# Other places in the order of work for three token pieces and one early load, in a bucket-attention and rational feed-forward kernel

## The chip, the core and the metric

The kernel runs on one core of a Trainium2 chip. The metric is device microseconds for one execution, lower being better. The five engines of the core each work through their own instructions in order: PE (TensorE, the matrix multiplications), DVE (VectorE), ACT (ScalarE), POOL (GpSimd) and SP (SyncE), which here does nothing but issue DMAs. They meet only through semaphores, so an instruction that waits holds up everything behind it on its engine.

## The reference: what is computed

Attention among tokens that fall into the same hash bucket, then a feed-forward layer with a rational function in its middle. Everything is float32.

```python
# q, k, v: 4 batches x 8 heads x 768 tokens x 64;  proj: 64 x 6
q_bits = (q @ proj > 0); k_bits = (k @ proj > 0)
q_bucket = sum(q_bits * 2**arange(6)); k_bucket = sum(k_bits * 2**arange(6))
scores = q @ k.T / sqrt(64)
scores = where(q_bucket[:, None] == k_bucket[None, :], scores, -1e9)
attn = exp(scores - max(scores)); attn = attn / (sum(attn) + 1e-9)
x = (attn @ v)                       # heads side by side: 3072 tokens x 512
# feed-forward, w_in: 512 x 2048, w_out: 2048 x 512
h = x @ w_in
P = a[0] + a[1]*h + a[2]*h**2 + a[3]*h**3
Q = 1 + abs(b[0])*abs(h) + abs(b[1])*h**2
out = (P / (Q + 1e-6)) @ w_out       # 3072 x 512
```

## The kernel before, in words

**Precision.** A float32 operand of a matmul is split into a high part (a rounded copy, made by ACT) and a low part (the operand less its high part, made by DVE or POOL), and the products of high with high, high with low and low with high are added up. Names ending in `1`, `_hi`, `h` are high parts, those ending in `2`, `lo`, `_lo`, `l` low ones.

**Attention.** The 32 heads are handled as 16 pairs (0 to 15), two heads on the 128 partitions. For a pair, `load` brings q and k (`qkf<-qT`, `qkf<-kT`, 384 KB each) into a tile that two pairs share in turn; `high` and `low` split them; `second_low` and `second_high` copy the halves to where the second of the two score matmuls reads them, eight DMAs of 192 KB within the chip; `bits` multiplies q and k by the projection for two pairs at once (`psb`, for pairs 2 and 3 in one go), and `penalties` and `maskrows` turn the bits into extra rows of q and k, so that the mask is part of the score product. `maxstep` (`psm` on PE, `m` on DVE) finds each query's largest score, `shift_turn` and `shift_rows` make it one more row. Then come twelve steps, `scores` (`pss` on PE, the exponential `E` on ACT, and running sums `acc` on POOL, for the last pair half of them on DVE) and, for six steps together, `values` (`psv`, 24 matmuls, which read all six exponentials). The results go to `x_d` in memory, the reciprocal sums to `r_d`.

**Weights.** Beside all this, `weights(0)` to `weights(31)` bring in w_in (even numbers) and w_out (odd ones) in blocks of 512 KB (`wr<-w_in`, `wr<-w_out`; 64-bit values, which ACT and DVE turn into float32) and split them; w_out's go back to memory as `wo_d`. The blocks 28 to 31 fall into the last two pairs.

**Feed-forward.** Tokens are taken in 6 blocks of 512. Each block's 512 features for 512 tokens are loaded in three pieces by `Tokens.load(t, c)`: pieces 0 and 1 are 768 wide, piece 2 is 512 wide. A piece takes four steps: DMAs for x and its reciprocal sums r (six for pieces 0 and 1, three for piece 2; all on SP); the multiplication `x<-x,r` on DVE; the high part `xh` on ACT; the low part `xl` on DVE. x and r lie in one buffer each (tags `lo0` and `lo1`, which `low` also uses during attention), so a piece's DMAs wait until the piece before has been read for the last time. `psh` and `pso` are the two products. The first block's pieces are made during the pairs 14 and 15; this change-over, from about 360 to 420 us, is called the seam here.

**Order.** Every engine keeps the program order. That order is written out in a table: each piece of work is entered under a number (12 times the pair plus a step with decimals), and the program is put out in rising numbers. The dictionaries `MID`, `FIRST` and `LAST` hold these numbers. `LAST["tokens"]` holds four numbers for each of the three pieces, counted from pair 15, `FIRST["load3"]` the one for the load of pair 3, counted from pair 0. No cost model or due time is at work when the program is built; moving a number moves the work past its neighbours on each engine that it uses.

```python
for g in sorted(plan):
    for f, args in plan[g]:
        f(*args)
```

Of the kernel before, what the change touches and what calls it, by code (L numbers as in the profile page):

```python
# [50 lines left out]
    maxima1=4.62, rate1=0.45, maxima2=9.5, rate2=0.82, high=[3.25, 3.53], low=[6.0, 7.3], bits=7.15, penalties=7.25,  # L51
    high_move=4.53, maskrows=8.2, second_low=4.25, second_high=4.35, load_v=4.78, group=2,
    values=[2.35, 2.65, 2.32, 2.35, 0.35, 0.61], values_out=3.02, high1=[-0.27, -5.58], low1=[11.24, 4.95],
    high_move1=20.05, load2=21.89, load3=4.5, penalties1=-6.57, maskrows1=3.69,
    weights=[[-5.7, 6.64, 6.7, 11.42, 12.19, 18.75, 21.75, 38.77, 44.13], [8.03, 9.04, 9.24, 11.12, 14.81, 15.27, 15.99, 17.91, 46.81]],
    warm=6, warms=[3, 3, 3, 1, 1, 1], maxima00=[-4.26, -2.29, -4.17, 1.67, -1.15, 2.77], shift00=[2.15, 4.99],
    shift0=[3.67, 3.44], ahead=3, scores=[[3.68, 3.82, 7.26], [6.03, 8.25, 12.4]], pen01=[4.77, 14.55], comp01=3.35,
# [3 lines left out]

LAST = dict(
    group=6, values=[0.28, 0.44], values_out=1.39, vout14=3.03,
    tokens=[[-11.0, -7.43, -6.5, -5.11], [-3.0, 0.9, 2.1, 3.83], [4.9, 8.5, 9.38, 9.53]], terms=7.05, ffn=[13.61, 16.09, 16.14],
    sums=16.96, wide=8, share=11, third=0, sums14=14.69, sumst14=22.46,
)
TINY = 2.0 ** -80
# [764 lines left out]
```

## Time and profile before

| | us |
|---|---|
| median of 3 runs | 942.82 (941.68 to 946.25) |
| the profiled execution itself | 940.38 |
| its span in the profile | 938.6 |
| PE busy | 924.1 (98%) |
| DVE busy | 840.5 (90%) |
| ACT busy | 647.0 (69%) |
| POOL busy | 436.0 (46%) |

The profile comes from one execution, and its times count from the start of the span. In the rows below, `out<-in` gives the tiles by the program's names, `xN` says how many instructions a row stands for, and a bracket at the end gives how long the engine sat idle before the row and what ended that. All instructions have one line number (93), as a helper records them; the tiles tell them apart. `SPq` rows are the issues of DMAs on SP's queue, not the transfers. A row with several instructions is a merged one: its start is that of the first, and its length runs to the modelled end of the last.

### The profile page before, as it was taken

What the parts mean: (1) busy time and instruction counts of PE and PEld (TensorE: products, weight loads), DVE (VectorE), ACT (ScalarE), POOL (GpSimd) and SP (SyncE); (2) the same over time, 40 slices, a digit from 0 to 9 for tenths busy, and PEclk for the clock granted to TensorE, in tenths of its full rate; (3) what the DMA queues carried; (4) which work ended last, traced back from release to release, by engine and by line L of the source; (5) the groups of instructions that cost most, each with busy time, mean ns of one, the idle gap of its engine ahead of it and who ended that gap; (6) DMA issues with size and microseconds to landing.
All of it is one profiled execution on the core that took longest, in us unless ns stands there. A gap on an engine that the chain in (4) does not pass through costs nothing.

```text
span 938.6 us, 13660 instructions
## 1 busy us (share of the span) xinstructions
PE 924.1 (98%) x4678; PEld 700.4 (75%) x4678; DVE 840.5 (90%) x1029; ACT 647.0 (69%) x1229; POOL 436.0 (46%) x362
## 2 busy tenths in 40 slices
PE   8899999999999999999999999999999999999997
PEld 4466766676766766568888888888888888888886
DVE  6699889888988897789998999899999999998996
ACT  6466767676776766777777676777687677667664
POOL 5467888888778776622222222222322322222222
PEclk9999999999999999999999999999999999999999
DMA  6667878777878776536401100210021002001001
GB/s 195 175 181 229 226 218 228 215 223 225 229 223 227 227 193 197 170 119 246 142 29 62 51 23 1 79 35 23 1 79 38 20 34 79 23 1 45 0 1 45
DMA packets 51242, 111.57 MB, mean 119 GB/s; under 512 B 9346, under 2 KB 20214, under 8 KB 51172
## 3 DMA queue, kind: packets, MB, share of 16 engines
q1 hardware_dynamic: 50740, 110.47, 39.6%
q8 instruction: 37, 0.61, 0.3%
q14 instruction: 33, 0.27, 0.1%
q10 hardware_dynamic: 432, 0.23, 0.1%
HBM read 56.82 MB, written 21.17 MB: 83 GB/s over the span
## 4 chain that ended last, share of the span: by engine, by line
PE 89%; DVE 5%; DMA 2%; ACT 1%; issue 1%; SPq 1%; ACTq 0%; DVEq 0%
PE psh L93 28%; PE pso L93 28%; PE pss L93 12%; PE psv L93 11%; PE psm L93 6%; DVE m L93 3%; PE psu L93 2%; PE psb L93 1%; DVE ws L93 1%; ACT E L93 1%; SPq L93 1%; DMA qkf<-kT 1%; DVE wr L93 1%; DVE lo L93 1%; DMA q<-q 1%
## 5 line engine op out<-in xcount | busy, mean ns | idle before, releaser
L93 POOL TENSOR_TENSOR gl<-c,gh 128x512 fp32r<-128x512 f32 x96 | 136.4, 1421 | 385.8 <-ACT gh L93 376.5
L93 ACT ACTIVATE E<-pss 128x384 f32<-128x384 f32 x384 | 167.4, 492 | 107.2 <-PE pss L93 91.0
L93 PE MATMUL pso<-wo,gh 128*128 128x512 f32 x768 | 235.6, 389 | 0.0
L93 DVE TENSOR_REDUCE m<-psm 128x1 f32<-128x768 f32 x192 | 179.3, 948 | 34.0 <-PE psm L93 31.0
L93 POOL TENSOR_TENSOR acc<-E,E 128x384 f32<-128x384 f32 x124 | 152.9, 1252 | 91.8 <-ACT E L93 91.6
L93 PE MATMUL pss<-q,k 128*128 128x384 f32 (+2 forms) x768 | 171.1, 347 | 0.3 <-ACT E L93 0.3
L93 PEld LDWEIGHTS pso<-wo,gh 128*128 128x128 f32 x768 | 144.2, 188 | 29.9
L93 PEld LDWEIGHTS pss<-q,k 128*128 128x128 f32 (+2 forms) x768 | 134.7, 190 | 28.9 <-issue 17.0
L93 ACT ACTIVATE h<-psh 128x512 f32<-128x512 f32 x96 | 57.4, 598 | 135.0 <-PE psh L93 134.8
L93 PE MATMUL psh<-xh,wi_hi 128*128 128x512 f32 x384 | 149.8, 390 | 0.0
L93 PE MATMUL psh<-xl,wi_hi 128*128 128x512 f32 x384 | 149.6, 390 | 0.0
L93 PE MATMUL psh<-xh,wi_lo 128*128 128x512 f32 x384 | 149.6, 390 | 0.0
L93 PE MATMUL pso<-wo,gl 128*128 128x512 f32 x384 | 148.6, 389 | 0.0
L93 POOL TENSOR_TENSOR acc<-acc,E 128x384 f32<-128x384 f32 x123 | 136.5, 1128 | 13.5 <-ACT E L93 13.4
L93 DVE SCALAR_TENSOR_TENSOR c<-c,ab,r 128x512 f32<-128x512 f32 x96 | 139.7, 1456 | 0.0
L93 PE MATMUL psv<-E,v 128*64 128x385 f32 x768 | 133.7, 492 | 1.6 <-ACT E L93 1.6
L93 PE MATMUL psm<-k,q 76*128 76x384 f32 (+1 forms) x384 | 102.5, 349 | 2.2 <-DVE m L93 1.0
L93 PEld LDWEIGHTS psv<-E,v 128*64 128x64 f32 x768 | 52.7, 137 | 68.3 <-issue 61.5
L93 DVE SCALAR_TENSOR_TENSOR w<-h,absb,w 128x512 f32<-128x512 f32 x96 | 72.8, 759 | 15.7 <-ACT w L93 15.4
L93 PEld LDWEIGHTS psh<-xh,wi_hi 128*128 128x128 f32 x384 | 72.1, 188 | 16.1 <-issue 1.2
L93 PEld LDWEIGHTS psh<-xh,wi_lo 128*128 128x128 f32 x384 | 72.1, 188 | 14.9
L93 PEld LDWEIGHTS pso<-wo,gl 128*128 128x128 f32 x384 | 72.1, 188 | 14.9
(78 smaller groups left out, 1217.7 us busy)
## 6 DMA issues: line engine op xcount, KB each, us to landing
q<-q SPq DMA_DIRECT2D x45, 192.0 KB
k<-k SPq DMA_DIRECT2D x45, 192.0 KB
wr<-w_in SPq DMA_DIRECT2D x16, 512.0 KB
wr<-w_out SPq DMA_DIRECT2D x16, 512.0 KB
wo_d<-wr SPq DMA_DIRECT2D x16, 512.0 KB
wo<-wo_d SPq DMA_DIRECT2D x16, 512.0 KB
qkf<-qT SPq DMA_DIRECT2D x16, 384.0 KB
qkf<-kT SPq DMA_DIRECT2D x16, 384.0 KB
```

What stands on the lines that cost most here:

```text
L93: return self.tc.keep_in_program_order(issue(*args, **kwargs))
```

## The change

Two sets of numbers in the table of the order.

The load of pair 3 moves from 4.5 to 3.8. On SP's queue its two DMAs stood behind pair 1's `second_low` and `second_high`; now they stand in front of these, directly behind the four DMAs of pair 1's mask rows.

The three token pieces of the first feed-forward block get new numbers for their steps (only the last step of piece 2 keeps its own). In the order of the program:

- piece 0: its DMAs, which stood before weight block 28, pair 15's `second_high` and pair 13's second store, now stand behind these and before pair 13's sums. Its multiplication moves on DVE behind two maximum steps and two steps of block 28; its `xh` on ACT behind the exponentials of pair 14's steps 6 to 9, block 28's high part and pair 14's first output; its `xl` on DVE behind `shift_turn` of pair 15, the low part of block 28 and a step of block 29.
- piece 1: its DMAs move behind pair 15's load of v, before block 30. Its multiplication moves from step 0 of pair 15 to step 3; its `xh` from before the high part of block 29 to behind block 30's two conversions, just before the exponential of pair 15's step 5; its `xl` behind that step's add and a step of block 30.
- piece 2: its DMAs, its multiplication, its `xh` and its `xl` keep their neighbours on each engine (the numbers differ, but no other work of the same engine lies between), except that its DMAs can start only once piece 1's `xl` has been done.

No instruction is added or taken away.

```diff
 FIRST = dict(
...
-    high_move1=20.05, load2=21.89, load3=4.5, penalties1=-6.57, maskrows1=3.69,
+    high_move1=20.05, load2=21.89, load3=3.8, penalties1=-6.57, maskrows1=3.69,
...
 LAST = dict(
     group=6, values=[0.28, 0.44], values_out=1.39, vout14=3.03,
-    tokens=[[-11.0, -7.43, -6.5, -5.11], [-3.0, 0.9, 2.1, 3.83], [4.9, 8.5, 9.38, 9.53]], terms=7.05, ffn=[13.61, 16.09, 16.14],
+    tokens=[[-7.43, -5.11, -2.83, -1.09], [-0.04, 3.83, 4.5, 5.2], [6.0, 9.38, 9.45, 9.53]], terms=7.05, ffn=[13.61, 16.09, 16.14],
```

## The prediction

> **What bounds the kernel now.** I read the page first, then busy time by stretch, then the engines' timelines at the two places the change touches.
>
> ```profile
> span 938.6 us, 13660 instructions
> PE 924.1 (98%) x4678; PEld 700.4 (75%) x4678; DVE 840.5 (90%) x1029; ACT 647.0 (69%) x1229; POOL 436.0 (46%) x362
> ```
>
> PE is busy for 98% of the span, so only its 14.5 us of gaps can be won, and what every gap drags behind it. The busy time by stretch says where they lie:
>
> ```profile
> 0.00:50.00 50.00, 43.97 (x222) 24.38 (x222) 30.06 (x46) 27.03 (x46) 24.12 (x31) 1.00 0.66 191
> ...
> 200.00:250.00 50.00, 50.00 (x313) 34.20 (x313) 45.69 (x55) 36.01 (x82) 40.17 (x35) 1.00 0.80 233
> ...
> 380.00:400.00 20.00, 18.86 (x112) 11.62 (x111) 13.61 (x18) 14.39 (x34) 12.14 (x11) 1.00 0.57 184
> ```
>
> Columns: stretch, length, then busy us (count) of PE, PE's weight loads, DVE, ACT, POOL, then granted clock, DMA share, GB/s. The gaps are in the first 50 us and at the seam around 380 to 400, where attention passes into the feed-forward part; each of the two edits lies in one of them. In between PE is full, so what it gains early should arrive at the end undiminished.
>
> **Part 1, the load of pair 3 (load3, 4.5 to 3.8).** PE's timeline in pair 0:
>
> ```profile
> 33.92 0.84 PE L93 MATMUL psb<-qkf,prj 128*32 128x384 f32 x4
> ...
> 38.58 1.48 PE L93 MATMUL psb<-qkf,prj 128*32 128x384 f32 x10 [1.61 <-DMA qkf<-kT]
> 39.99 1.51 PE L93 MATMUL psv<-E,v 128*64 128x385 f32 x8
> ```
>
> These 16 matmuls make the bucket bits of pairs 2 and 3 together, and wait twice for pair 3's q and k. Here they hold PE from 33.92 to 39.99, 6.07 us; undisturbed, in the chain of waits, they take 1.29:
>
> ```profile
> 82.89 1.29 PE psb L93 x16
> ```
>
> So 6.07 - 1.29 = 4.78 us is the most this part can give. SP's queue, in its order of issue:
>
> ```profile
> 26.23 1.17 SPq L93 DMA_DIRECT2D q<-lo  x2
> ...
> 30.01 1.43 SPq L93 DMA_DIRECT2D k<-k  x2
> 31.54 0.94 SPq L93 DMA_DIRECT2D qkf<-qT  x1
> 32.53 0.81 SPq L93 DMA_DIRECT2D qkf<-kT  x1
> ```
>
> The two loads move ahead of eight copies within the chip (pair 1's low and high halves, two to a row from 26.23 to 31.44), from 31.54 to 26.23, 5.31 us sooner. Their tile is free by then: its last reader is POOL's subtraction of pair 1.
>
> ```profile
> 20.98 1.84 POOL L93 TENSOR_TENSOR lo<-qkf,q 128x768 fp32r<-128x768 f32 x1
> ```
>
> When do they land? Before, k was issued at 32.53 and released PE at 38.58, 6.05 us later, with eight copies in front. Issued at 27.22 (26.23 plus the 0.99 between the two), even that long a time gives 33.27, before PE asks at 33.92; a shorter one changes nothing. Both waits go. The eight copies start 1.8 us later and behind the loads' bytes. POOL's next subtraction overwrites the low half that they copy out; a delay there is some 3 us at most (the loads' 1.8 of issue and what their bytes take) and meets POOL alone, busy for 46% of the span. Pair 1's scores, which read the copies, come only when pair 0's twelve steps are through, long after.
>
> I take 4.7 of the 4.78; the bounds are 0 (a new wait at once, below) and 4.78. Less than 0 is excluded here: the same bytes are queued from 26.23 on, so the last of them is no later than before.
>
> **Part 2, the token pieces at the seam.** Five breaks of PE lie there:
>
> ```profile
> 372.14 3.45 PE L93 MATMUL psv<-E,v 128*64 128x385 f32 x20
> 376.14 1.25 PE L93 MATMUL psv<-E,v 128*64 128x385 f32 x4 [0.54 <-ACT E L93]
> 377.31 0.98 PE L93 MATMUL pss<-q,k 77*128 77x384 f32 x4
> ...
> 380.86 0.28 PE L93 MATMUL pst<-cst,m 128*12 128x128 f32 x1 [0.48 <-DVE m L93]
> ...
> 383.19 4.10 PE L93 MATMUL psv<-E,v 128*64 128x385 f32 x24
> 387.22 2.38 PE L93 MATMUL pss<-q,k 77*128 77x384 f32 x12
> ...
> 397.42 1.24 PE L93 MATMUL psv<-E,v 128*64 128x385 f32 x4 [0.65 <-ACT E L93]
> 398.59 4.05 PE L93 MATMUL pss<-q,k 77*128 77x384 f32 x20
> 402.94 0.97 PE L93 MATMUL pss<-q,k 77*128 77x384 f32 x4 [0.30 <-ACT E L93]
> ...
> 407.69 1.24 PE L93 MATMUL psv<-E,v 128*64 128x385 f32 x4 [0.39 <-ACT E L93]
> ```
>
> An undisturbed block of 24 takes 387.22 - 383.19 = 4.03. The block at 372.14 took 5.17 until 377.31: a gap shown as 0.54 costs 1.14, since the pipeline refills. Reckoned likewise, the breaks at 380.86, 397.42, 402.94 and 407.69 cost about 1.0, 1.3, 0.8 and 1.0: 5.2 us in all, the most part 2 can give.
>
> The first two have one cause:
>
> ```profile
> 363.82 0.33 SPq L93 DMA_DIRECT2D x<-x_d  x1
> ...
> 368.51 0.59 SPq L93 DMA_DIRECT2D wr<-w_in  x1
> ...
> 383.31 1.07 SPq L93 DMA_DIRECT2D x<-x_d  x1
> ...
> 388.01 0.43 SPq L93 DMA_DIRECT2D wr<-w_in  x1
> ...
> 394.59 0.33 SPq L93 DMA_DIRECT2D x<-x_d  x1
> ...
> 400.58 0.34 SPq L93 DMA_DIRECT2D wr<-w_out  x1
> ```
>
> Piece 0's six DMAs (363.82) stand ahead of weight block 28 (368.51). ACT, in order, waits for that block and holds pair 14's exponentials behind it:
>
> ```profile
> 374.44 0.68 ACT L93 ACTIVATE ws<-wr 128x512 f32<-128x512 f32 x1 [3.02 <-DMA wr<-w_in]
> ...
> 392.59 0.84 ACT L93 CAST xh<-x 128x768 fp32r<-128x768 f32 x1 [1.29 <-DVE x L93]
> ...
> 395.71 0.72 ACT L93 ACTIVATE ws<-wr 128x512 f32<-128x512 f32 x1
> ...
> 406.00 0.69 ACT L93 ACTIVATE ws<-wr 128x512 f32<-128x512 f32 x1
> ```
>
> With piece 0 moved behind the high copies and pair 13's store, block 28 takes their place at 363.8. With its own old time from issue to use, 374.44 - 368.51 = 5.93, it is there at 369.7; ACT asks at 374.44 - 3.02 = 371.42. The 3.02 vanish, and DVE's 3.0 of idle behind them, which had made the transposition at 380.86 late. Gain 1.14 + 1.0, of which I give back 0.6, as PE now runs up to the exponential that frees its score buffer: 1.5 at 383.19.
>
> The rest works the other way. Piece 0's low part (xl) now comes behind block 29's step on DVE, which waits for ACT:
>
> ```profile
> 384.14 0.94 DVE L93 TENSOR_SCALAR wr<-wr 128x512 int32<-128x512 int32 x1 [1.04 <-ACT ws L93]
> ...
> 391.60 0.96 DVE L93 TENSOR_TENSOR x<-x,r 128x768 f32<-128x768 f32 x1 [2.00 <-DMA r<-r_d]
> ...
> 397.84 1.35 DVE L93 TENSOR_TENSOR acc<-acc,E 128x384 f32<-128x384 f32 x1
> ```
>
> It ends at about 385.2, and piece 1 needs that one tile: its six DMAs go at 385.2 instead of 383.31, block 30 behind them at 389.2 instead of 388.01. ACT, free of the 1.29 wait and of the cast at 392.59 (now later), wants block 30 at 395.71 - 1.29 - 0.84 - 1.5 = 392.1. Behind it come two conversions, piece 1's cast and the first half of the exponential that PE's block waits for, some 2.3 us by ACT's starts, then 1.17 for the block's last four (397.42 to 398.59). With the time L from a block's issue to its use: at 3.6 (block 31: the DMA engines fell idle 3.6 after 400.58, as below) block 30 is there at 392.8 and PE's block ends at 396.3; at 5.93 it is there at 395.1, and the block ends at 398.6: 2.2 or 0 us ahead of before. Piece 1's xl stands behind pair 15's add (397.84) and a weight step now, some 3 us after that exponential, so piece 2 issues at 398.2 to 400.5 rather than 394.59, and block 31, behind it and one store, at 400.1 to 402.4 against 400.58. ACT takes it at 406.00 less the lead. At L = 3.6 it is in time and the lead stays, 2.2; at 5.93 it is there at 408.3, 2.3 late.
>
> ```profile
> 404.00:405.00 1.00, 1.00 (x8) 0.46 (x8) 1.00 (x3) 0.28 (x1) 0.00 (x0) 1.00 0.13 46
> ```
>
> So part 2 lies between -2.2 and +2.3. Block 30 has less in front of it than block 28 had, and block 31 little: I put L at 4.3 and 3.8, near the lower end, which makes -1.5, and take -1.3. Moves past pair 15's v load and pair 13's sums cost nothing: v is issued sooner, the sums are read after the seam only.
>
> The moved subtractions and multiplies read two SBUF tiles, with POOL's adds beside them. DVE's add at 397.84, 384 wide, took 1.35, where half of the 768-wide multiply at 391.60 would be 0.48: 0.87 more. I leave that out of the sum, since which of the moved ones meet an add can't be told from before, and make it a rival. The Trainium skill, "SBUF — State Buffer", section "Who interferes with whom", has such a rule, and it speaks against this change: a DVE instruction with two SBUF inputs and a GpSimd one that reads SBUF shut each other out for a whole instruction. The 1.35 agrees with it.
>
> **The sum.** 4.7 + 1.3 = 6.0. The profiled execution took 940.38 (span 938.6 and 1.78 around it), so 934.4; the median of 942.82 lies 2.44 above it, so **936.8**.
>
> **Rivals.**
>
> *Seam nothing, pair 0 as forecast*: the two xl meet POOL's adds, 0.87 each; both stand in the chain to block 31, which is 1.7 later. 942.82 - 4.7 - 1.3 + 1.7 = 938.5. For it: the 1.35. Against: POOL does only every second add of pair 15's, as DVE takes the others.
>
> *A wait in the place of the one removed*: pair 2's mask rows wait for ACT, then ride the DMA queue, and PE reads them at 48.31, in the changed kernel at 48.31 - 4.78 = 43.5; the w_out block issued behind them all, and the copies in front, fill the queue until about 41 and the four issues take 0.8 each, so they land between 43 and 46.5.
>
> ```profile
> 42.20 0.80 SPq L93 DMA_DIRECT2D q<-mb  x1
> ```
>
> ```profile
> 48.31 0.98 PE L93 MATMUL psm<-k,q 76*128 76x384 f32 x4
> ```
>
> At 46.5 part 1 keeps 4.7 - 3.0 = 1.7; with 1.3 at the seam that is 3.0, 939.8. At 43 nothing is lost. The Trainium skill's page "DMA: Bandwidth & Descriptors", section "Queues, rings and completion order", speaks for the wait: each DMA engine consumes its descriptors in ring order, so the small rows stay behind the large loads.
>
> *Everything vanishes*: 4.8 + 5.2 = 10, 932.8. Against it: the late block 30.
>
> *Slower*: the chain piece 0's xl, piece 1's DMAs, block 30, exponential, piece 1's xl, piece 2's DMAs, block 31, all through one tile and one queue. Each us of L beyond 5.93 costs 2, as both blocks are late. From +2.3 it outweighs 4.7 at L = 7.1; at 8.3, what piece 1 itself took (383.31 to DVE's multiply at 391.60), the seam costs 7.0: 942.82 - 4.7 + 7.0 = 945.1. Against: 5.93 is the longest of the blocks seen.
>
> **Chances.** Forecast 0.50 (its own range 935.0 to 938.3), seam nothing 0.17, mask rows 0.17, everything 0.08, slower 0.08. A change under 0.5%, 4.7 us, can't be told from none: faster needs less than 938.1, all of the forecast but a little, the large gain, and the lower part of seam-nothing: 0.62; the same 0.31; slower 0.07. The range runs from 933.0 to 941.5, leaving out the slower case and part of the largest.
>
> **What would show it.** Right: psb x16 at 33.9 without waits, and pair 1's scores 4.7 sooner; ACT's wait at 374.44 (then near 367) gone; pst without wait. Wrong: a wait of psm on the mask rows near 43.5; ACT waiting for wr<-w_in or wr<-w_out at blocks 30 and 31; the end of the block at 407.69 less than 4.7 us ahead.

## The result, and the profile after

The changed kernel takes 937.08 us in the median (936.41 to 937.54, 9 runs), the kernel before beside it 942.65 (939.80 to 946.25, 9 runs): 0.994 of it, with a 95% interval of 0.9925 to 0.9956. Forecast were 936.8, within 933.0 to 941.5. The number was met; of the two parts that it was added up from, one was larger than forecast and the other had the wrong sign.

The head of the changed kernel's page, of the profiled execution of 937.44:

```profile
span 935.6 us, 13659 instructions
...
PE 922.6 (99%) x4678; PEld 701.4 (75%) x4678; DVE 840.5 (90%) x1029; ACT 648.5 (69%) x1229; POOL 436.6 (47%) x362
```

Busy time by stretch, with the columns of the prediction's second fence:

```profile
0.00:50.00 50.00, 47.02 (x251) 28.16 (x251) 36.21 (x52) 30.40 (x53) 29.09 (x35) 1.00 0.70 205
200.00:250.00 50.00, 49.06 (x297) 33.41 (x297) 42.28 (x54) 35.20 (x78) 38.51 (x33) 1.00 0.80 220
380.00:400.00 20.00, 17.85 (x98) 12.45 (x96) 14.60 (x16) 12.90 (x31) 8.77 (x8) 0.91 0.46 133
```

In the first 50 us PE is busy 3.05 longer than before. In the 20 us at the seam it is busy 1.01 less, at a granted clock of 0.91. Some 0.94 of gaps is new in the middle, near 200, where nothing was changed (PE waits 0.49 for v and 0.45 for an exponential); the changed kernel's second profile has no wait there, so it belongs to this execution.

**Pair 0.** PE's timeline, then SP's queue:

```profile
33.23 1.50 PE L93 MATMUL psb<-qkf,prj 128*32 128x384 f32 x16
34.66 1.51 PE L93 MATMUL psv<-E,v 128*64 128x385 f32 x8
...
42.98 0.98 PE L93 MATMUL psm<-k,q 76*128 76x384 f32 x4
```

```profile
25.56 0.52 SPq L93 DMA_DIRECT2D qkf<-qT  x1
26.13 0.42 SPq L93 DMA_DIRECT2D qkf<-kT  x1
26.59 1.18 SPq L93 DMA_DIRECT2D q<-lo  x2
```

Both waits in psb are gone: its 16 matmuls hold PE for 34.66 - 33.23 = 1.43 instead of 6.07, a gain of 4.64. PE reaches the values behind them 39.99 - 34.66 = 5.33 sooner; the other 0.69 is the start, which differs between executions (psb begins at 33.23 here, at 33.92 before). The product at 42.98 that reads pair 2's mask rows does not wait.

**The seam.** PE from the values of pair 14 to the first matmul of the feed-forward part:

```profile
367.28 4.10 PE L93 MATMUL psv<-E,v 128*64 128x385 f32 x24
...
373.92 0.27 PE L93 MATMUL pst<-cst,m 128*12 128x128 f32 x1
...
375.30 1.69 PE L93 MATMUL pss<-q,k 77*128 77x384 f32 x8 [0.39 <-ACT col L93]
...
387.00 3.45 PE L93 MATMUL psv<-E,v 128*64 128x385 f32 x20
392.61 1.24 PE L93 MATMUL psv<-E,v 128*64 128x385 f32 x4 [2.15 <-ACT E L93]
393.78 6.03 PE L93 MATMUL pss<-q,k 77*128 77x384 f32 x24
...
402.82 1.24 PE L93 MATMUL psv<-E,v 128*64 128x385 f32 x4 [0.27 <-ACT E L93]
404.70 1.25 PE L93 MATMUL psv<-E,v 128*64 128x385 f32 x4 [0.63 <-ACT E L93]
405.87 0.50 PE L93 MATMUL psh<-xh,wi_hi 128*128 128x512 f32 x1
```

The same last matmul in the kernel before:

```profile
408.86 0.50 PE L93 MATMUL psh<-xh,wi_hi 128*128 128x512 f32 x1
```

From the first values to the first `psh`, which the rest of this text calls the length of the seam, the changed kernel takes 405.87 - 367.28 = 38.59 and the kernel before took 408.86 - 372.14 = 36.72. The first two breaks of before are gone (the block at 367.28 takes 4.03 until 371.31, the transposition at 373.92 does not wait), but a larger one stands in front of 392.61, and two at the end. The small one at 375.30, where PE waits for ACT, is the one for which the prediction gave back 0.6. ACT, DVE and SP in the same stretch:

```profile
366.45 0.66 ACT L93 ACTIVATE ws<-wr 128x512 f32<-128x512 f32 x1
...
390.20 0.67 ACT L93 ACTIVATE ws<-wr 128x512 f32<-128x512 f32 x1 [2.74 <-DMA wr<-w_in]
...
401.76 0.62 ACT L93 CAST xh<-x 128x512 fp32r<-128x512 f32 x1 [2.45 <-DVE x L93]
402.29 0.87 ACT L93 ACTIVATE E<-pss 128x384 f32<-128x384 f32 x2
```

```profile
379.76 1.76 DVE L93 TENSOR_TENSOR xl<-x,xh 128x768 fp32r<-128x768 f32 x1
...
394.64 0.95 DVE L93 TENSOR_TENSOR xl<-x,xh 128x768 fp32r<-128x768 f32 x1
...
401.03 0.69 DVE L93 TENSOR_TENSOR x<-x,r 128x512 f32<-128x512 f32 x1 [1.29 <-DMA r<-r_d]
```

```profile
381.59 0.32 SPq L93 DMA_DIRECT2D x<-x_d  x1
...
384.90 0.58 SPq L93 DMA_DIRECT2D wr<-w_in  x1
...
395.66 0.32 SPq L93 DMA_DIRECT2D x<-x_d  x1
...
397.22 0.58 SPq L93 DMA_DIRECT2D wr<-w_out  x1
```

Block 28 is there without a wait (366.45). Piece 0's `xl` ends at 381.5, and piece 1's DMAs go at once (381.59). Block 30 goes behind them at 384.90, and ACT waits 2.74 for it at 390.20, 5.30 after its issue; that makes PE's break of 2.15. Then piece 2's reciprocal sums are late: DVE waits for r, ACT for DVE (2.45, at 401.76), and the exponentials of pair 15's steps 10 and 11 stand behind that cast. PE waits twice for them.

So the spans give: 5.33 ahead after psb, 372.14 - 367.28 = 4.86 ahead when the seam begins (a net 0.47 was lost on the way, near 200), 4.86 - 1.87 = 2.99 ahead when it ends, and 938.6 - 935.6 = 3.0 at the end. The medians differ by 5.57. Why the two differ is the last of the questions that the experiments take up.

### The profile page after: what moved, and what is told of

Read it like the earlier page. It is cut to its first block, busy times and chain, and to the rows that moved or that the text cites. A ratio compares the mean times of both kernels' runs of the same rounds, so it can differ in the third digit from the quotient of the medians.

```text
span 935.6 us, 13659 instructions
## 1 busy us (share of the span) xinstructions
PE 922.6 (99%) x4678; PEld 701.4 (75%) x4678; DVE 840.5 (90%) x1029; ACT 648.5 (69%) x1229; POOL 436.6 (47%) x362
## 4 chain that ended last, share of the span: by engine, by line
PE 91%; DVE 3%; DMA 3%; ACT 2%; SPq 1%; issue 1%; ACTq 0%; DVEq 0%
PE psh L93 28%; PE pso L93 28%; PE pss L93 13%; PE psv L93 12%; PE psm L93 7%; PE psu L93 2%; DMA wr<-w_in 2%; DVE m L93 2%; PE psb L93 1%; SPq L93 1%; ACT E L93 1%; DMA r<-r_d 0%; DMA qkf<-kT 0%; DVE ws L93 0%; DVE wr L93 0%
## 5 line engine op out<-in xcount | busy, mean ns | idle before, releaser
L93 DVE SCALAR_TENSOR_TENSOR c<-c,ab,r 128x512 f32<-128x512 f32 x96 | 135.6, 1413 | 0.0
L93 PEld LDWEIGHTS psh<-xl,wi_hi 128*128 128x128 f32 x384 | 72.1, 188 | 14.9
```

Of the source, the lines that this page charges most:

```text
L93: return self.tc.keep_in_program_order(issue(*args, **kwargs))
```

## The experiments

**Each part alone.** First the load alone, in the kernel before:

```diff
-    high_move1=20.05, load2=21.89, load3=4.5, penalties1=-6.57, maskrows1=3.69,
+    high_move1=20.05, load2=21.89, load3=3.8, penalties1=-6.57, maskrows1=3.69,
```

> The kernel before with pair 3's load at 3.8 and the token pieces at their old places. Theory (the forecast's part 1): both waits of psb vanish, 4.7 us, so a median 4.7 below the kernel before's beside it, and a seam like the one before (breaks worth about 5 us). Rival (the shift is partly eaten later on by a wait for v or the mask rows): less than 3.5 us below, with a wait of PE between 43 and 345 us that the kernel before does not have.

Measured: 936.52 (935.33 to 940.19), 0.9954 of the kernel before, interval 0.9936 to 0.9972. psb holds PE for 35.34 - 33.91 = 1.43, as in the changed kernel; the seam takes 36.82, as before.

Then the tokens alone:

```diff
-    tokens=[[-11.0, -7.43, -6.5, -5.11], [-3.0, 0.9, 2.1, 3.83], [4.9, 8.5, 9.38, 9.53]],
+    tokens=[[-7.43, -5.11, -2.83, -1.09], [-0.04, 3.83, 4.5, 5.2], [6.0, 9.38, 9.45, 9.53]],
```

> The kernel before with the three token pieces at their new places and pair 3's load at 4.5. Forecast's part 2: 1.3 us below the kernel before. What the profile of the changed kernel says instead: its lead of 6.3 us at the 24 psv before the last pair's first values shrinks to 3.0 at the first psh, so the pieces gain 1.4 us on the first half of the seam and lose 3.3 on the second, 1.9 slower than before. The one wants 1 to 1.5 us below, the other 1.5 to 2.5 above. If the second is right, ACT waits 2.5 to 3 us for wr<-w_in at block 30, PE then about 2 us for E.

Measured: 941.50 (939.71 to 946.67), 1.0006, interval 0.9987 to 1.0024. The time is neither of the two that were expected, but the interval reaches to 2.3 us above the kernel before. The seam takes 38.84, with the breaks of the changed kernel:

```profile
396.51 1.24 PE L93 MATMUL psv<-E,v 128*64 128x385 f32 x4 [2.47 <-ACT E L93]
...
406.65 1.25 PE L93 MATMUL psv<-E,v 128*64 128x385 f32 x4 [0.91 <-ACT E L93]
408.55 1.24 PE L93 MATMUL psv<-E,v 128*64 128x385 f32 x4 [0.65 <-ACT E L93]
```

The load carries all that was gained. The new token places make the seam 2.1 longer in this profile, and no gain can be seen in the time.

**What makes block 30 late.** The next two kernels start from the changed one. In the first, piece 1's DMAs go behind block 30 on SP; in the second they do too, piece 0's `xh` and `xl` come sooner, and piece 1's `xh` stands behind the exponential of step 5 instead of in front of it.

```diff
-    tokens=[[-7.43, -5.11, -2.83, -1.09], [-0.04, 3.83, 4.5, 5.2], [6.0, 9.38, 9.45, 9.53]],
+    tokens=[[-7.43, -5.11, -2.83, -1.09], [1.5, 3.83, 4.5, 5.2], [6.0, 9.38, 9.45, 9.53]],
```

> The changed kernel with piece 1's DMAs behind weight block 30 on SP instead of in front (number 1.5 instead of -0.04). Theory (SP's queue: the block is held behind piece 1, whose tile comes free late): ACT's wait of 2.74 us for wr<-w_in goes, and PE's 2.15 before the last four psv shrinks below 1.2, as only piece 1's multiplication (ready near 390) still holds xh; 1.5 to 3 us below the changed kernel's 937.1. Rival (the DMA engines' throughput, not the order, sets when piece 1 and block 30 are in): the wait moves to xh for the same 2 to 3 us and the time stays within 0.7 us of 937.1.

Measured: 934.89 (933.45 to 939.51), 0.9936, interval 0.9917 to 0.9954; seam 36.02. ACT takes block 30 without a wait.

```diff
-    tokens=[[-7.43, -5.11, -2.83, -1.09], [-0.04, 3.83, 4.5, 5.2], [6.0, 9.38, 9.45, 9.53]],
+    tokens=[[-7.43, -5.11, -3.9, -3.3], [1.5, 3.83, 5.05, 5.2], [6.0, 9.38, 9.45, 9.53]],
```

> As the run before, and piece 0's xh and xl earlier (-3.9 and -3.3 instead of -2.83 and -1.09, so xl no longer stands behind block 29's step on DVE) and piece 1's xh behind the exponential of pair 15's step 5 instead of before it. Theory: piece 1's six DMAs issue about 4 us sooner (near 378 instead of 381.6), nothing waits for block 30 or piece 1, the 20+4 psv of pair 15 run without a break, and the granted clock stays at 1.00 around 394: 4 to 6 us below the changed kernel's 937.1, so 931 to 933. Rival (ACT's own work, not its waits, holds the exponentials): the break before the last four psv stays over 1 us and the time is above 935.

Measured: 934.55 (933.14 to 938.16), 0.9929, interval 0.9905 to 0.9953; seam 35.37. The block of values in which the changed kernel broke off runs through in 4.10 (4.74 in the kernel ahead). The time falls short of the 931 to 933 expected: the last two breaks stay, 0.50 and 0.64 here, 0.52 and 0.63 there, with ACT waiting 2.44 and 2.46 in front of piece 2's cast. To tell the edits apart, a third kernel moved only piece 0's `xh` and `xl` and left block 30 behind piece 1's six DMAs:

```diff
-    tokens=[[-7.43, -5.11, -2.83, -1.09], [-0.04, 3.83, 4.5, 5.2], [6.0, 9.38, 9.45, 9.53]],
+    tokens=[[-7.43, -5.11, -3.9, -3.3], [-0.04, 3.83, 4.5, 5.2], [6.0, 9.38, 9.45, 9.53]],
```

> The changed kernel with piece 0's xh and xl before block 29's steps and pair 14's first output, and nothing else; piece 1's DMAs still stand ahead of block 30. Theory (piece 0's late xl, 379.8 plus 1.76 beside POOL's add, is what makes piece 1's DMAs, and through SP's order block 30, late): piece 1's DMAs go near 378 instead of 381.6 and block 30 near 381.8 instead of 384.9; with its 5.3 to 5.6 from issue to use it is there at 387.1 to 387.4, when ACT asks for it (387.4), so the waits of 2.74 on ACT and 2.15 on PE are gone; the end of the seam still waits for piece 2 (0.5 and 0.64). Seam 38.6 to between 35.4 and 36.2, median 934.5-936. Rival (block 30 is late because the six DMAs stand ahead of it, whenever they go): ACT's wait stays over 1.5, the seam over 37.5.

Measured: 933.53 (932.70 to 935.35), 0.9909, interval 0.9886 to 0.9932, below what was expected; seam 401.66 - 365.95 = 35.71. Its DVE, SP, ACT and PE:

```profile
374.66 1.18 DVE L93 TENSOR_TENSOR xl<-x,xh 128x768 fp32r<-128x768 f32 x1 [1.31 <-ACT xh L93]
```

```profile
380.27 0.58 SPq L93 DMA_DIRECT2D wr<-w_in  x1
```

```profile
385.97 0.73 ACT L93 ACTIVATE ws<-wr 128x512 f32<-128x512 f32 x1
```

```profile
385.67 4.10 PE L93 MATMUL psv<-E,v 128*64 128x385 f32 x24
...
398.62 1.25 PE L93 MATMUL psv<-E,v 128*64 128x385 f32 x4 [0.87 <-ACT E L93]
400.49 1.24 PE L93 MATMUL psv<-E,v 128*64 128x385 f32 x4 [0.63 <-ACT E L93]
```

Counted from the seam's start, `xl` ends at 375.84 - 365.95 = 9.89 instead of 381.52 - 367.28 = 14.24, and block 30 goes at 14.32 instead of 17.62. ACT takes it without a wait, and the block at 385.67 runs unbroken. So block 30 was late because it stood behind six DMAs that had to wait for piece 0's late `xl`. Either edit is enough: with block 30 in front the wait goes, and with an early `xl` it is in time behind the six DMAs too.

**What holds up the end of the seam.** Piece 2's `xh` and `xl` were put behind the exponential of step 11, in the changed kernel alone, in the second kernel above (with piece 0's `xl` early), and there once more with piece 1's `xh` and `xl` and piece 2's DMAs sooner still. The changed kernel ran beside them.

```diff
-    tokens=[[-7.43, -5.11, -2.83, -1.09], [-0.04, 3.83, 4.5, 5.2], [6.0, 9.38, 9.45, 9.53]],
+    tokens=[[-7.43, -5.11, -2.83, -1.09], [-0.04, 3.83, 4.5, 5.2], [6.0, 9.38, 11.1, 11.2]],
```

> The changed kernel with piece 2's xh and xl behind the exponential of step 11 and nothing else. Theory (two losses in a row: block 30 late costs the first, piece 2's xh in front of the exponentials the second): the break of 2.15 in front of the first block's last four stays, the waits of 0.27 and 0.63 at the end shrink; the exponential of step 10 near 399.8 instead of 402.29, that of step 11 behind block 31 (issued at 397.22) at 402.0 to 403.7 instead of 404.17. Seam 38.6 to between 37.0 and 38.2; 0.4 to 1.6 us below the changed kernel. If block 30 were all, nothing moves.

> The changed kernel once more, beside the three others on one chip. The part that comes from pair 0 (4.7 us) stands, and the seam gives nothing back: 936.5 to 937.5, 0.993 to 0.996 of before; its profile shows a seam of 38 to 39 us, with the break for block 30 and one at the end. If the break of 2.15 for block 30 was a chance of one execution, the seam is near 36.5.

Measured: 936.46 (935.06 to 939.88), 0.9947, interval 0.9926 to 0.9968, beside 937.01 (936.08 to 939.24), 0.9951, interval 0.9934 to 0.9968, for the changed kernel, whose break for block 30 came again (2.41). The seams take 37.69 and 38.71. The last 24 values with piece 2 behind, and ACT's step in front of exponential 11:

```profile
400.98 4.70 PE L93 MATMUL psv<-E,v 128*64 128x385 f32 x24
```

```profile
402.73 0.70 ACT L93 ACTIVATE ws<-wr 128x512 f32<-128x512 f32 x1 [1.18 <-DMA wr<-w_out]
```

The two breaks are gone but for 0.6, and a wait for block 31 shows, which had been hidden behind the cast. The times of the two can't be told apart; the shorter seam rests on the profile.

```diff
-    tokens=[[-7.43, -5.11, -2.83, -1.09], [-0.04, 3.83, 4.5, 5.2], [6.0, 9.38, 9.45, 9.53]],
+    tokens=[[-7.43, -5.11, -3.9, -3.3], [1.5, 3.83, 5.05, 5.2], [6.0, 9.38, 11.1, 11.2]],
```

> As the run with piece 0's xl early, but piece 2's xh and xl stand behind the exponential of step 11; its DMAs stay. Theory: the wait of 2.44 for DVE's x is no longer in front of the exponentials; the exponential of step 10 runs near 396.3 instead of 399.19, the break of 0.50 in front of the first four last values goes. The exponential of step 11 then waits for weight block 31, issued at 394.45: there at 398.1 with 3.6 us, at 399.8 with 5.3, plus 1.24 for its two conversions: 399.3 to 401.0 instead of 401.07. So the seam falls from 35.4 to between 33.8 and 34.9, the median to 933.0-934.1. Rival (want of scores or of ACT's time): nothing moves, 934.5.

Measured: 933.89 (932.25 to 934.53), 0.9912, interval 0.9893 to 0.9931; seam 34.46. The break for exponential 10 is gone, and that for exponential 11 has grown to 0.85, again for block 31, which is used 4.60 after its issue at 395.51:

```profile
400.11 0.68 ACT L93 ACTIVATE ws<-wr 128x512 f32<-128x512 f32 x1 [2.04 <-DMA wr<-w_out]
```

```diff
-    tokens=[[-7.43, -5.11, -2.83, -1.09], [-0.04, 3.83, 4.5, 5.2], [6.0, 9.38, 9.45, 9.53]],
+    tokens=[[-7.43, -5.11, -3.9, -3.3], [1.5, 3.83, 4.05, 4.12], [4.9, 9.38, 11.1, 11.2]],
```

> Early piece 0, block 30 first, piece 1's xl right behind block 30's steps, piece 2's DMAs early and its xh and xl behind the exponential of step 11. Theory (piece 2's xh, waiting for a late r, holds back the exponentials of pair 15's steps 10 and 11): piece 1's xl ends some 2 us sooner than the 392.81 of the run with the xl early, so piece 2's DMAs and block 31 go near 390.5 and 392; block 31 is there at 396 to 397.5, the exponentials 10 and 11 run as soon as PE has made their scores, and the last two blocks of four follow without a break. The seam (first values of pair 14 to first psh) falls from 35.4 to 33.0-33.8 us and the median to 932-933. Rival (the last exponentials are late for want of PE's scores or of ACT's own time, whatever stands among them): the breaks 0.50 and 0.64 stay, the seam stays at 35, the median at 934.5. Third way: piece 2 comes too late for the first psh now (its third group of three reads it, 2.0 us after the first psh): psh would show a wait on xh or xl of up to 1.5.

Measured: 932.87 (931.83 to 934.81), 0.9907, interval 0.9888 to 0.9926; seam 34.05, a little above what was expected, since a wait of 1.60 for block 31 is left on ACT and a break of 0.43 on PE. Nothing waits for piece 2 in the feed-forward part. It is the lowest time of this study, though not to be told from the 933.53 above.

**Why the medians differ by more than the spans.** All kernels with the early load ran in 931.8 to 940.2 us, those with the old one in 938.5 to 946.7. The kernel before was profiled twice more, unchanged.

> The kernel before, unchanged, for a second profiled execution. Its runs spread over 938.5 to 946.3 us, those of every kernel with the early load over 931.8 to 940.2, and the one that was profiled (940.38) lies 2 under the median. If the wait for pair 3's load is what spreads, an execution near 942.5 holds psb's 16 matmuls about 2 us longer than the 6.07, and PE reaches the values behind them near 42 instead of 39.99. Rival: psb ends at 39.99 plus or minus 0.3 again, and the time is lost elsewhere (around 200 us, where two executions of other kernels lost 1.4, or at the seam, 36.72 before).

> A third execution of the kernel before, on the same question: if its time differs from the others' by d, the theory has the end of psb differ by about d, the rival has it at 39.99 plus or minus 0.3.

Measured: 941.23 and 942.54. PE in pair 0, in the first and in the second of them:

```profile
36.04 1.49 PE L93 MATMUL psb<-qkf,prj 128*32 128x384 f32 x2 [1.95 <-DMA qkf<-qT]
38.48 2.77 PE L93 MATMUL psb<-qkf,prj 128*32 128x384 f32 x10 [0.95 <-DMA qkf<-kT]
41.17 1.55 PE L93 MATMUL psv<-E,v 128*64 128x385 f32 x4
```

```profile
37.99 1.49 PE L93 MATMUL psb<-qkf,prj 128*32 128x384 f32 x2 [3.64 <-DMA qkf<-qT]
40.16 2.77 PE L93 MATMUL psb<-qkf,prj 128*32 128x384 f32 x10 [0.68 <-DMA qkf<-kT]
42.86 1.72 PE L93 MATMUL psv<-E,v 128*64 128x385 f32 x8
```

And busy time by stretch in the same two (PEclk, the granted clock, is the third number from the end):

```profile
38.00:40.00 2.00, 1.52 (x9) 0.55 (x10) 0.00 (x0) 0.00 (x0) 0.00 (x0) 0.50 1.04 319
```

```profile
38.00:40.00 2.00, 1.48 (x2) 0.17 (x2) 0.00 (x0) 0.00 (x0) 0.00 (x0) 0.50 1.02 245
```

PE's values behind psb start at 41.17 and 42.86, not at 39.99 plus or minus 0.3: the rival falls. The theory's size was near, and too small for the execution that took about 942.5: psb holds PE for 9.35 there (from 33.51), 3.28 above the 6.07 where about 2 was expected, and for 7.92 (from 33.25) in the one of 941.23. The times differ from the first profile's by 0.85 and 2.16, the starts of the values by 1.18 and 2.87. q's wait is 1.37 to 3.64 long, and in these two executions the clock is at half when the ten matmuls behind it run, so that they take 2.77 instead of 1.48.

Taken together, the profiled executions fall into two terms. The rest is the execution's time less the start of the values behind psb:

| | execution | values behind psb | rest | seam |
|---|---|---|---|---|
| before | 940.38 | 39.99 | 900.39 | 36.72 |
| before, second | 941.23 | 41.17 | 900.06 | 36.71 |
| before, third | 942.54 | 42.86 | 899.68 | 36.96 |
| load alone | 936.97 | 35.34 | 901.63 | 36.82 |
| load alone, again | 934.43 | 34.26 | 900.17 | 37.07 |
| tokens alone | 941.25 | 39.23 | 902.02 | 38.84 |
| changed | 937.44 | 34.66 | 902.78 | 38.59 |
| changed, again | 937.25 | 35.34 | 901.91 | 38.71 |

The load alone was timed twice; beside the second of these profiles:

> The load of pair 3 alone once more, on the chip and beside the run of the kernel before of this call. If the token pieces' new places cost what the seams of the profiles say (about 2), this is 935-936.5 and the changed kernel, 937.0 in both its timings, is the slower of the two by 0.5 to 2; if they are worth nothing either way, 936.5-937.5.

Measured: 934.76 (933.63 to 935.51), 0.9918, interval 0.9898 to 0.9938; its 0.9954 above and the changed kernel's 0.9940 and 0.9951 lie around it, so the times do not say which of the two kernels is the faster. All six runs of this second timing (933.63 to 935.51) lie below the eight of the changed kernel's second (936.08 to 939.24), but those of the load's first timing (935.33 to 940.19) do not. The profiles say more of the parts. With the old token places the seam takes 36.71 to 37.07 (five executions), with the new ones 38.59 to 38.84 (three): 1.9 more, and the rest of the execution is 1.85 longer on average. With the old load the values behind psb start at 39.23 to 42.86 (four), with the new one at 34.26 to 35.34 (four).

## Why the number was right, and which step was wrong

**Part 1.** The mechanism was right, in each link: no wait in psb, no wait on the mask rows, pair 1's scores 5.3 sooner (at 48.18 instead of 53.50), the lead kept to the seam but for 0.47. Against the profiled execution it gave 4.64, where 4.7 was put; the bound of 4.78 took 1.29 for the undisturbed matmuls, which hold PE for 1.43. What was mis-sized is the bound: "4.78 us is the most this part can give" holds for that execution only. psb held PE for 6.07, 7.92 and 9.35 in three executions of the kernel before and for 5.32 with the tokens alone, against 1.43, so the part is worth 3.9 to 7.9, on average 5.7.

**Part 2, first half.** Right: block 28 comes without a wait, both breaks are gone. The changed kernel starts its block of values at 387.00, 387.00 - 367.28 = 19.72 into the seam, the kernel before at 393.28 - 372.14 = 21.14: 1.4 gained, where 1.5 was put.

```profile
393.28 3.49 PE L93 MATMUL psv<-E,v 128*64 128x385 f32 x20
```

**Part 2, block 30.** The chain was the right one, but two of its sizes were not. Counted from the start of the seam, the prediction had piece 1's DMAs at 385.2 - 372.14 = 13.06 and block 30's issue at 389.2 - 372.14 = 17.06; they came at 14.31 and 17.62. Of the delay 0.81 is `xl`, which took 1.76 beside POOL's adds, where that of piece 1, at 394.64 with POOL idle, took 0.95. POOL in the changed kernel at that time:

```profile
378.55 2.15 POOL L93 TENSOR_TENSOR acc<-E,E 128x384 f32<-128x384 f32 x2
380.67 1.73 POOL L93 TENSOR_TENSOR acc<-acc,E 128x384 f32<-128x384 f32 x1
```

This is what the rival "seam nothing" priced at 0.87, and it met one `xl` of two. The Trainium skill, "SBUF — State Buffer", section "Who interferes with whom", has the rule that a DVE instruction with two SBUF inputs contends with a GpSimd one that reads SBUF, and the 1.76 beside 0.95 agrees with it. The other is L. "Block 30 has less in front of it than block 28 had" is where the step failed: block 30 stands behind six DMAs of a piece just as block 28 did with its 5.93, and needed 5.30, and 5.56 in the changed kernel's other profile, where 4.3 was put. So block 30 was used at 390.20 - 367.28 = 22.92 instead of 17.06 + 4.3 = 21.36, 1.56 later: 0.56 from the issue and 1.00 from L. The block of values ended 393.78 - 367.28 = 26.50 into the seam, before 398.59 - 372.14 = 26.45. The 1.4 was given back.

**Part 2, the end.** This is the step that failed outright. The prediction looked for the next loss at block 31, and had piece 2's DMAs later, but put nothing in the sum for what piece 2 itself would hold up, and gave no reason; the text ahead of it says that its steps keep their neighbours. Its DMAs start 395.66 - 393.78 = 1.9 after the block of values has ended instead of 4.0 before (394.59 to 398.59), and its `xh` stands on ACT in front of two exponentials. From the end of the block to `psh` the changed kernel takes 405.87 - 393.78 = 12.09, the kernel before 408.86 - 398.59 = 10.27: 1.8 lost. With the cast behind the exponentials it was 10.75, beside 11.29 for the changed kernel's second profile, and 10.31 in the kernel of the lowest time, which has piece 2's DMAs early as well. Block 31 was in time only because ACT stood at piece 2's cast in front of it; with the cast moved away its own wait shows (1.18, 2.04 and 1.60). Its L of 4.60 to 5.00 was put at 3.8, from an issue that had no piece's DMAs right in front of it. In the order of issue, one thing also differs from what the text ahead of the prediction says: the store of block 29 stands in front of piece 2's DMAs, not behind them.

So part 2 cost 1.9 and not -1.3, 3.2 off, and close to its upper bound of 2.3. Two of the signs of being wrong that the prediction named showed it: ACT's wait for block 30, and an end of the seam that was 2.99 ahead instead of 4.7.

**The sum.** The number was met by luck: two errors cancel. 2.44 was added to both kernels for what the median lies above the profiled execution. The changed kernel's profiled execution lies 0.36 above its own median, so nothing of the kind was to be added there; the kernel before lies higher in part since its wait in psb can be longer than in the one execution that was read, as its two other profiles show. On average 7.16 - 1.43 = 5.73 for the load less 1.85 for the tokens makes 3.9 of the 5.3 to 5.6 that the medians show. The rest, about 1.5, lies in executions that were not profiled, and the runs don't show where: the profiled executions of the old load average 941.35, about 1 below the medians.

**The rivals.** The mask rows do not wait: issued from 37.95 to 40.51, they are there when PE reads them at 42.98. "Everything vanishes" is refuted by the late block 30, as was said against it. The chain of the slower case is real in all its links, but L stayed under 5.93, so it did not outweigh the load. "Seam nothing" named one of the causes and was nearest on the seam.

## What to carry to other kernels

When a piece of work keeps its neighbours in the order but what feeds it has been made later, price it like a moved one, and ask on each engine what stands behind it: a cast that waits for a late DMA in front of an exponential costs the exponential's reader. Take the time from issue to use from a transfer with the same load right in front of it in the queue. And where a wait for a DMA is to be removed, look at it in more than one execution: here what it held up varied by 4 us, and the three profiled executions of the kernel before differed by that and hardly by anything else.

## What the runs showed of the hardware

The granted clock fell in or after short waits of PE. In the changed kernel, behind the break of 2.15:

```profile
394.00:395.00 1.00, 1.00 (x5) 1.00 (x5) 1.00 (x3) 0.49 (x1) 0.00 (x0) 0.65 0.05 16
395.00:396.00 1.00, 1.00 (x5) 1.00 (x4) 1.00 (x2) 0.91 (x3) 0.00 (x0) 0.50 0.00 0
396.00:397.00 1.00, 1.00 (x4) 1.00 (x4) 0.19 (x1) 0.81 (x3) 0.03 (x1) 0.50 0.36 49
397.00:398.00 1.00, 1.00 (x5) 1.00 (x5) 0.70 (x1) 1.00 (x3) 0.98 (x1) 0.64 0.86 291
```

The clock is half from 394.31 to 397.72, for 3.41 us, beginning 1.7 us after PE had resumed at 392.61. The half lasts 3.41 us in the changed kernel's second profile and in the one with piece 2 behind too, and 6.83, twice that, in pair 0 of the kernel before's second and third profile, where it begins before q is there (at 35.91 with PE resuming at 36.04, and at 36.49 with PE resuming at 37.99). The 24 score products at 393.78 take 6.03 for it, where 20 took 4.05 before. With the tokens alone a wait of 2.47, at 396.51, left the clock at 1.00:

```profile
398.00:399.00 1.00, 1.00 (x7) 1.00 (x6) 1.00 (x3) 0.60 (x2) 0.00 (x0) 1.00 0.01 0
```

The seam was no shorter for it (38.84), as PE then waited longer for the exponentials; so at the seam the slower clock cost nothing that can be seen. In pair 0 it did: after waits of 1.95 and 3.64, the ten matmuls behind the second wait took 1.29 more. The Trainium skill, "TensorE: Matmul & The Clock Gate", section "Part 1: The HAM clock gate (the "warmup" mystery)", has the clock halve after an idle window of about 3.4 us and come back after a busy one of that length; the halving and the 3.41 agree, while here a wait of 1.95 was enough in one execution and 2.47 was not in another.
